# A fused attention and feed-forward kernel: the opening loads, tables and warm-up rearranged, and two blocks of the first chunk moved behind the second

## The chip, the cores and the metric

The program runs on one core of one Trainium2 chip. The metric is the device time of one execution in microseconds, and less is better. The core has a matrix engine (PE, with a loader of its stationary operands, PEld), a vector engine (DVE), a scalar engine (ACT), a general engine (POOL), and a queue engine (SP) that issues most of the DMA transfers.

## What is computed

Windowed causal attention with a distance bias, and a feed-forward layer on its output, all in float32:

```
B, H, S, D = 8, 8, 576, 64;  window = 128
scores = q k^T / sqrt(D) + slope_h * -|rel|, only for 0 <= rel < window
attn   = softmax(scores)                      # minus the row maximum, sum + 1e-9
x      = (attn v), heads side by side         # 4608 tokens x 512
h = x @ w_in                                  # 512 -> 2048
g = h * erf(softplus(h))
out = g @ w_out                               # 2048 -> 512
```

## The kernel before

The 4608 tokens are cut into 12 chunks of 384 tokens. Chunk c has four attention units, u = 4c to 4c+3, each for two heads. In each group of three chunks the last (units 8 to 11, 20 to 23, ...) joins the tails of two batches. Of a unit, PE makes the scores `s` (L464), DVE adds the bias and finds the row minimum (L491, six instructions and six small reads of accumulators), ACT takes the exponentials (L501), DVE inverts the sums (L514, L515), POOL scales the probabilities `p` (L524), PE transposes them into `t` (L543), DVE or ACT copies `t` into `pT`, PE multiplies by the values into `px` (L576), ACT or DVE writes the rounded half of x, and DVE the rest of x (L586), which is the last reader of `px`.

Products of the feed-forward layer are made in three passes of rounded operands (high by high, high by low, low by high). The first pass over the chunks uses the first six of the 16 column blocks of w_in and w_out: per chunk and block, 12 products into `h` (L783, six for each half of x), then softplus and erf on ACT, the split of g on DVE (L825 to L830), and nine products into three accumulators `o0` to `o2` (L846). After a chunk's sixth block the accumulators are copied and stored to DRAM (`keep_part`). The remaining ten blocks are worked in a second pass (L985, L1056), which loads these parts again and adds them (`store`).

The weights arrive as 64-bit floats. Each block of w_in or w_out is decoded by one ACT instruction and five DVE instructions (L621, L623, L625, L626, L631; tiles `wqi`, `wti`, for w_out `wqo`, `wto`), rounded (L638), and its remainder taken on DVE (L641). Twelve such blocks are prepared at the start of the kernel, beside the first attention units.

PE writes into PSUM banks: three under the tag `a` (scores, transposes and `px`), two for `h`, three for `o`. While the `h` and `o` banks are still unused, the scores of the first SPARE units go there (`early`). The scores of a unit that joins two batches take three banks, from unit 8 on all three `a` banks at once:

```
        ps = [bank(j) for j in range(2 + (last and len(ts) == 3))]
```

The order of the instructions on each engine is not that of the code. `Plan.run` is a list scheduler that runs when the program is built: it keeps modelled clocks of the engines and the DMA, and at each moment gives an engine the ready operation with the smallest `at`, if its buffers are free. The `at` of a unit is `unit_time(u)`, that of first-pass work counts up from LEAD in steps of TM, that of the weights is set in `prepare`. On the chip each engine then runs its list strictly in order, and an instruction that waits holds up all behind it on that engine. The warm-up products (L397, 40 pairs of matmuls on zeros) have the largest `at` and fill moments in which PE has nothing else.

Of the kernel before, what the change touches and what calls it, by code (L numbers as in the profile page):

```python
# [44 lines left out]
LL, LN, LT = 26, 0, 0  # L45
SQ = 0.36
# [59 lines left out]
class Plan:  # L106
# [254 lines left out]
class Attention:  # L361


    def __init__(self, tc, plan, ctx, actx, qk, v, bias, ident, moe):
        self.nc, self.plan = tc.nc, plan
        self.qk, self.v = qk, v
        self.ident, self.moe = ident, moe
        nc, op = self.nc, plan.op
        sb = lambda name: actx.enter_context(tc.tile_pool(name=name, bufs=1))
        biases = sb("biases")  # L370
        self.bias = []
        rel = Buf(shape=[P, 4, D], ap=biases.tile([P, 4, D], F32, name="rel"))
        op(emit=lambda e: nc.scalar.dma_start(rel.all, bias), w=[rel], at=-9, **dma(P * 4 * D * 4, run=1024, eng="Act"))
# [32 lines left out]
    def load(self, u):  # L406


        c, g = u // 4, u % 4
        nc, op = self.nc, self.plan.op  # L410
        at = unit_time(u) - LL
        last = c % 3 == 2
        n, m = (640, 10) if last else (448, 6)
        i = c // 3 if last else c - c // 3
        src, vsrc = self.qk[last][i, g], self.v[last][i, g]
        qk = Buf(self.kp, [P, CH + 640], F32, "qk", NKB, f"qk{u}")
        v = Buf(self.vp, [P, 10, 2, D], F32, "v", NQ, f"v{u}")
        rows = lambda j: slice(j * D, (j + 1) * D)
        q = lambda t, j, h: qk[rows(j), t * P + h * D : t * P + (h + 1) * D]
        k = lambda j, x, w: qk[rows(j), CH + x : CH + x + w]  # L420
        if u:
            parts = [[qk]] * 3
            op(emit=lambda e: nc.sync.dma_start(qk[:, : CH + n], src), w=[qk], at=at, **dma(P * (CH + n) * 4, run=(CH + n) * 4))
        else:
            pieces = [Part(qk, i) for i in range(4)]
            for i, (eng, issue, lo, hi) in enumerate((
                    ("SP", nc.sync, 0, P), ("Act", nc.scalar, CH, CH + 192), ("Act", nc.scalar, CH + 192, CH + n), ("SP", nc.sync, P, CH))):
                op(emit=lambda e, issue=issue, lo=lo, hi=hi: issue.dma_start(qk[:, lo:hi], src[:, lo:hi]), w=[pieces[i]], at=-30 + i,
                   **dma(P * (hi - lo) * 4, run=(hi - lo) * 4, eng=eng))
# [288 lines left out]
class Moe:  # L718
# [117 lines left out]
    def products(self, u, j, gh, gl):  # L836
# [363 lines left out]
```

## Time and profile before

| | us |
|---|---|
| three runs | 1003.12, 1003.21, 1004.44 |
| median | 1003.21 |
| the profiled execution | 1003.54 |
| its span, first to last instruction | 1001.5 |
| PE busy | 987.4 |
| DVE busy | 687.2 |
| ACT busy | 666.8 |
| POOL busy | 157.1 |

The span is cut into stretches below, since shares over the whole span mix stages with different limits. The chain of waits goes back from the last instruction to what released each step, so it names the engine that set the pace at each moment. The granted clock is 1.00 of full speed in all 40 slices of the span that the page shows, and the rows' PEclk is that of the clock record, which begins some 5 us into the span.

### The profile page before, as it was taken

How to read it: one execution, taken by the hardware profiler on the slowest of the kernel's cores; microseconds unless marked ns; L12 is line 12 of the kernel's file. 1: busy time of each engine (PE TensorE's matmuls, PEld its weight loads, DVE VectorE, ACT ScalarE, POOL GpSimd, SP SyncE). 2: the span in 40 equal slices, each digit the busy share in tenths (PEclk: the TensorE clock that was granted, in tenths of full speed). 3: DMA queues.
4: the chain of work that ended last, by engine and by line, in shares of the span. 5: the costliest groups of instructions: out<-in, count | busy, mean ns of one | idle time of the engine just before them, and what ended most of it. 6: DMA issues, size and time to landing. Idle time of an engine off the chain costs nothing.

```text
span 1001.5 us, 17129 instructions
## 1 busy us (share of the span) xinstructions
PE 987.4 (99%) x6188; PEld 876.5 (88%) x6188; DVE 687.2 (69%) x1635; ACT 666.8 (67%) x1259; POOL 157.1 (16%) x294
## 2 busy tenths in 40 slices
PE   8899999999999999999999999999999999999998
PEld 7788988988888898888999898998989989889896
DVE  5999988999988966575647367457547547544433
ACT  6899788778788787667866555555455464564652
POOL 3543333223332532022000000000000000000000
PEclk9999999999999999999999999999999999999999
DMA  9654577768776754562985252241342441420402
GB/s 360 250 173 165 198 258 253 274 232 322 264 233 220 269 175 138 176 211 84 346 320 187 81 189 88 70 175 67 105 158 64 126 152 48 147 95 1 127 1 73
DMA packets 63508, 172.17 MB, mean 172 GB/s; under 512 B 7104, under 2 KB 7744, under 8 KB 63424
## 3 DMA queue, kind: packets, MB, share of 16 engines
q1 hardware_dynamic: 62992, 170.72, 49.1%
q8 instruction: 49, 0.80, 0.3%
q10 hardware_dynamic: 432, 0.36, 0.1%
q14 instruction: 35, 0.29, 0.1%
HBM read 118.88 MB, written 52.17 MB: 171 GB/s over the span
## 4 chain that ended last, share of the span: by engine, by line
PE 92%; DVE 5%; ACT 1%; DMA 1%; issue 1%; POOL 0%; POOLq 0%; DVEq 0%; ACTq 0%
PE o L846 15%; PE h L783 14%; PE pa L985 13%; PE po L1056 12%; PE pa L1056 12%; PE px L576 7%; PE pc L985 6%; PE s L464 5%; PE t L543 4%; PE pb L985 3%; DVE p L491 1%; PE warm_ps L397 1%; DMA wd<-wto 1%; ACT p L501 1%; POOL p L524 0%
## 5 line engine op out<-in xcount | busy, mean ns | idle before, releaser
L524 POOL TENSOR_SCALAR p<-p,st 128x192 f32<-128x192 f32 (+1 forms) x288 | 156.4, 563 | 305.2 <-DVE st L515 224.0
L783 PE MATMUL h<-x,wi 128*128 128x384 f32 x864 | 173.9, 343 | 0.1
L766 ACT COPY hs<-pa 128x384 f32<-128x384 f32 x93 | 44.7, 481 | 177.3 <-PE pa L985 176.7
L783 PEld LDWEIGHTS h<-x,wi 128*128 128x128 f32 x864 | 149.5, 188 | 8.8 <-issue 4.7
L501 ACT ACTIVATE p<-p,st 128x192 f32<-128x192 f32 (+1 forms) x288 | 124.1, 434 | 32.1 <-DVE st L491 31.9
L846 PE MATMUL o<-wo,gh 128*128 128x512 f32 x432 | 142.0, 410 | 0.0
L985 PE MATMUL pa<-t,p 128*128 128x384 f32 x540 | 108.9, 336 | 0.0
L576 PEld LDWEIGHTS px<-pT,v 128*128 128x128 f32 x704 | 101.2, 191 | 5.1 <-issue 1.1
L576 PE MATMUL px<-pT,v 128*128 128x192 f32 (+2 forms) x704 | 102.9, 295 | 0.7 <-ACT pT L402 0.6
L985 PEld LDWEIGHTS pa<-t,p 128*128 128x128 f32 x540 | 96.4, 188 | 5.9
L768 DVE COPY hs<-pa 128x384 f32<-128x384 f32 x27 | 15.1, 557 | 111.3 <-PE pa L985 111.3
L1056 PE MATMUL po<-ho,gh 128*128 128x512 f32 x270 | 91.0, 391 | 0.0
L1056 PE MATMUL pa<-ho,gh 128*128 128x512 f32 x270 | 90.5, 389 | 0.0
L846 PEld LDWEIGHTS o<-wo,gh 128*128 128x128 f32 x432 | 74.9, 189 | 13.5 <-issue 5.0
L846 PE MATMUL o<-wo,gl 128*128 128x512 f32 x216 | 85.4, 395 | 0.0
L1056 PE MATMUL po<-ho,gl 128*128 128x512 f32 x180 | 71.3, 396 | 0.0
L1056 PE MATMUL pa<-ho,gl 128*128 128x512 f32 x180 | 70.1, 389 | 0.0
L491 DVE CUSTOM_DVE_ANT_0 p<-s,bias 128x192 f32<-128x192 f32 x224 | 66.0, 350 | 5.2 <-PE s L464 4.8
L996 DVE TENSOR_TENSOR hs<-pc,hs 128x384 f32<-128x384 f32 x60 | 33.3, 555 | 52.0 <-PE pc L985 39.2
L1036 DVE TENSOR_TENSOR hs<-s,hs 128x768 f32<-128x768 f32 x60 | 56.3, 950 | 16.9 <-ACT s L1028 16.9
L543 PE MATMUL t<-ident,p 128*128 128x128 f32 x400 | 61.4, 275 | 4.8 <-POOL p L524 3.2
L464 PE MATMUL s<-qk 64*64 64x192 f32 (+1 forms) x1152 | 59.7, 322 | 3.3 <-ACT pT L402 0.8
(257 smaller groups left out, 1851.7 us busy)
## 6 DMA issues: line engine op xcount, KB each, us to landing
xd<-x SPq DMA_DIRECT2D x24, 768.0 KB, 5.6
qk<-qk_a SPq DMA_DIRECT2D x31, 416.0 KB, 4.6
v<-v_a SPq DMA_DIRECT2D x32, 384.0 KB, 3.8
v<-v_c SPq DMA_DIRECT2D x16, 640.0 KB, 4.0
pd<-ot SPq DMA_DIRECT2D x36, 256.0 KB, 3.2
out<-pd SPq DMA_DIRECT2D x36, 256.0 KB, 3.8
p<-wd SPq DMA_DIRECT2D x35, 256.0 KB, 5.0
wri<-w_in SPq DMA_DIRECT2D x16, 512.0 KB, 7.0
```

The costliest lines, as they stand in the source:

```text
L464: nc.tensor.matmul(bank[h * D : (h + 1) * D, x : x + n], lhsT=q(t, j, h), rhs=k(j, off[h], n), start=True, stop=True)
L491: nc.vector.tensor_tensor_reduce(out=pt[:, c0:, j, :], in0=ps[j][0][:, ps[j][1] : ps[j][1] + n].rearrange("p (c d) -> p c d", d=D), in1=se ...
L501: nc.scalar.activation(dst, dst, AF.Exp, bias=low[t][:, j : j + 1], scale=-1.0, accum_out=sums[t][:, j : j + 1])
L524: nc.gpsimd.tensor_scalar(dst, dst, sums[t][:, j : j + 1], 1.0, op0=ALU.mult, op1=ALU.mult)
L543: nc.tensor.matmul(two[:, :, (2 - cb) * D : (3 - cb) * D], lhsT=p[t][:, cb].rearrange("p j d -> p (j d)"), rhs=self.ident[:, :], is_transp ...
L576: nc.tensor.matmul(px[:, to : to + m * D], lhsT=v[:, blk].rearrange("p j d -> p (j d)"), rhs=run(src, m, 256)[:, :, :D], start=first and x ...
L766: self.nc.scalar.copy(out, src)
L783: nc.tensor.matmul(ps[:, :CH], lhsT=ww[:, cs], rhs=xx[:, k], start=(k2 + k + n == 0), stop=(k2 + k + n == 4),)
L846: nc.tensor.matmul(po.all, lhsT=g[:, j, cs], rhs=w.all, start=(u["start"] and n == 0), stop=(u["end"] and n == 2),)
L985: nc.tensor.matmul(dst[:, :CH], lhsT=wv[i](k), rhs=xb[l][:, k], start=start and k + n == 0, stop=k + n == 3, skip_group_check=not start)
L1036: op({"DVE": dve(2 * CH)}, lambda e, s=s, hs=hs: V.tensor_tensor(hs.all, s.all, hs.all, ALU.mult), r=[s, *parts], w=parts, at=at, port=True)
L1056: nc.tensor.matmul(po.all, lhsT=g[:, k, cs], rhs=w.all, start=start and n == 0, stop=end and n == 2)
```

## The change

- **First loads.** Unit 0's q and k come in one load on SP where four went over two queues; the bias pattern `rel` goes first on ACT's queue. The loads of q and k of units 0 to 3 are placed ahead of all others, and the values' loads have times of their own (VE, VL).
- **Bias tables.** ACT multiplies `rel` by the slopes for head pair 0 alone; POOL makes the tables of pairs 1 to 3, two instructions each.
- **Warm-up and banks.** The warm-up has 30 pairs of matmuls where 40 were, in bank `o1`. Five early units where four were, and a table TURN says which banks each of them takes.
- **p buffers.** Nine where eight were.
- **Pace of the units.** `unit_time` counts 4 us for each of the first 6 units and 6.5 for each after, where it was 4.5 for the first 10.
- **Turns.** Chunk 0 does blocks 0 to 3, then chunk 1 blocks 0 to 5, then chunk 0 blocks 4 and 5. Each of chunk 0's two turns fills the accumulators anew; at the second, `keep_part` loads the part that was stored at the first, adds it on DVE, and stores the sum.
- **The planner's model** counts 0.3 us where it counted 1.5 for what waits on a load that lands before its time 9 (TS).

```
-SPARE = 4
+SPARE = 5
-WARM = 40
+WARM = 30
-NQ, NKB, PB, XB, OB, TB = 2, 4, 8, 5, 5, 2
-TE, NE = 4.5, 10
+NQ, NKB, PB, XB, OB, TB = 2, 4, 9, 5, 5, 2
+TE, NE = 4, 6
+TURNS = ((0, 0, 4), (1, 0, 6), (0, 4, 6))
+TS, VL, NQF, SLP = 9, 8, 4, True
+WB, PIE = "o1", 2
+VE = -17
+TURN = (0, 1, 2, 1, 2, 1, 2, 1)
...
-            return 0.14 + LM
+            return 0.14 + (LM if o.end + o.lag > TS else 0.3)
...
-        op(emit=lambda e: nc.scalar.dma_start(rel.all, bias), w=[rel], at=-9, ...
+        op(emit=lambda e: nc.scalar.dma_start(rel.all, bias), w=[rel], at=-40, ...
...
-                    nc.scalar.mul(b[:, j], rel.all, 2.0 ** (2 - 2 * g - j))
-            op({"Act": 2 * act(4 * D)}, slopes, r=[rel], w=[b], at=unit_time(g) - LL + 6)
+                    slope = 2.0 ** (2 - 2 * g - j)
+                    if e == "Act":
+                        nc.scalar.mul(b[:, j], rel.all, slope)
+                    else:
+                        nc.gpsimd.tensor_scalar(b[:, j], rel.all, slope, 1.0, op0=ALU.mult, op1=ALU.mult)
+            op({"Pool": 2 * (0.24 + 4 * D * 0.00086)} if SLP and g else {"Act": 2 * act(4 * D)}, slopes, ...
...
-        banks = (...)[u % 3 if early else 0]
+        banks = (...)[TURN[u] if early else 0]
...
-        for c in range(self.nch):
+        begun = {c for c, _, _ in TURNS}
+        for c, lo, hi in [*TURNS, *((c, 0, NF1) for c in range(self.nch) if c not in begun)]:
...
-            for f in fs:
+            for f in fs[lo:hi]:
+                u["more"] = lo > 0
...
-        op({"DVE": dve(DM), "Act": act(DM, src=0.053)},
-           lambda e: self.copy(e, ot.all, po.all), r=[po], w=[ot], at=at)
+        if more:
+            op(emit=lambda e: nc.sync.dma_start(ot.all, part.ap), r=[part], w=[ot], at=at - 10, ...
+            op({"DVE": dve(DM)}, lambda e: nc.vector.tensor_tensor(
+                ot.all, po.all, ot.all, ALU.add), r=[po, ot], w=[ot], at=at)
+        else:
+            op({"DVE": dve(DM), "Act": act(DM, src=0.053)}, ...
```

With these numbers the scheduler writes another order on every engine. Three places follow, each before and now. The digits behind a name are the unit (s9, px8), the block (wo2) or the count of the chunk-and-block pairs (h6); the number after the underscore is a running one.

ACT at the start, before: the first loads and tables, then the exponentials of units 0 and 1 (p0, p1), then the first steps on the weights (wqi).

```order
L428 DMA qk0_230<-qk_a 128x256
L373 DMA rel_152<-bias 128x256
L379 ACTIVATE bias0_153<-rel_152 128x256 x2
L379 ACTIVATE bias1_154<-rel_152 128x256 x2
L379 ACTIVATE bias2_155<-rel_152 128x256 x2
L379 ACTIVATE bias3_156<-rel_152 128x256 x2
L501 ACTIVATE p0_0_304,st0_305<-p0_0_304,st0_305 128x2x64 x2
```

ACT at the start, now, from the load of `rel` to the first weight steps.

```order
L378 DMA rel_152<-bias 128x256
L386 ACTIVATE bias0_153<-rel_152 128x256 x2
L511 ACTIVATE p0_0_291,st0_292<-p0_0_291,st0_292 128x2x64 x2
L511 ACTIVATE p0_1_312,st0_292<-p0_1_312,st0_292 128x3x64 x2
L511 ACTIVATE p0_2_317,st0_292<-p0_2_317,st0_292 128x3x64 x2
L511 ACTIVATE p1_0_338,st1_339<-p1_0_338,st1_339 128x2x64 x2
L511 ACTIVATE p1_1_346,st1_339<-p1_1_346,st1_339 128x3x64 x2
L511 ACTIVATE p1_2_350,st1_339<-p1_2_350,st1_339 128x3x64 x2
L511 ACTIVATE p2_0_360,st2_361<-p2_0_360,st2_361 128x2x64 x2
L511 ACTIVATE p2_1_372,st2_361<-p2_1_372,st2_361 128x3x64 x2
L511 ACTIVATE p2_2_382,st2_361<-p2_2_382,st2_361 128x3x64 x2
L628 ACTIVATE wqi0_438<-wri0_245 128x512
```

Three tables are gone from ACT, and three units' exponentials stand ahead of the first weight step where two did.

DVE up to the x that unit 9's scores wait for, before: that of unit 7 (px7).

```order
L631 TENSOR_TENSOR wto1_983<-wto1_983,wqo1_965 128x512
L626 SCALAR_TENSOR_TENSOR wqo2_985<-wro2_388,wqo2_985 128x512
L638 CAST wo1_1094<-wto1_983 128x512
L825 TENSOR_TENSOR hs2_930<-s2_1013,hs2_930 128x768
L641 TENSOR_TENSOR wo1_1094<-wto1_983,wo1_1094 128x512
L631 TENSOR_TENSOR wto2_1017<-wto2_1017,wqo2_985 128x512
L514 TENSOR_SCALAR st8_1033<-st8_1033 128x6
L515 RECIPROCAL st8_1033<-st8_1033 128x6
L586 TENSOR_TENSOR x1_1_977<-px7_1085,x1_1_977 128x384
```

DVE up to the x that unit 9's scores wait for, now: that of unit 8 (px8).

```order
L641 TENSOR_TENSOR wto2_1060<-wto2_1060,wqo2_1049 128x512
L636 SCALAR_TENSOR_TENSOR wqo3_1051<-wro3_511,wqo3_1051 128x512
L648 CAST wo2_1128<-wto2_1060 128x512
L641 TENSOR_TENSOR wto3_1062<-wto3_1062,wqo3_1051 128x512
L651 TENSOR_TENSOR wo2_1128<-wto2_1060,wo2_1128 128x512
L648 CAST wo3_1136<-wto3_1062 128x512
L631 TENSOR_SCALAR wto4_1138<-wqo4_1115 128x512
L651 TENSOR_TENSOR wo3_1136<-wto3_1062,wo3_1136 128x512
L633 SCALAR_TENSOR_TENSOR wto4_1138<-wqo4_1115,wto4_1138 128x512
L596 TENSOR_TENSOR x2_0_1149<-px8_1117,x2_0_1149 128x384
```

Unit 8's x now stands between unit 7's and unit 9's scores, and blocks 2 and 3 of w_out, with steps of block 4, stand ahead of it.

PE just ahead of unit 9's scores, before.

```order
L586 MATMUL px7_1085<-pT7_1069,v7_896 128x64
L846 MATMUL o2_0_1100<-wo0_981,gh0_960 128x512 x2
L846 MATMUL o2_0_1100<-wo0_981,gl0_967 128x512
L783 MATMUL h7_1108<-x1_0_821,wi1_580 128x384 x6
L846 MATMUL o0_0_1071<-wo1_1094,gh0_960 128x512 x2
L846 MATMUL o0_0_1071<-wo1_1094,gl0_967 128x512
L464 MATMUL s9_02_1135<-qk9_656 64x192
```

PE just ahead of unit 9's scores, now.

```order
L586 MATMUL px8_1117<-pT8_1087,v8_1011 128x64
L795 MATMUL h5_982<-x1_1_1020,wi1_654 128x384 x6
L795 MATMUL h6_1152<-x1_0_907,wi2_726 128x384 x6
L474 MATMUL s9_02_1162<-qk9_609 64x192
L474 MATMUL s9_01_1164<-qk9_609 64x192
```

Unit 8's `px` has moved ahead of unit 9's scores, with one half of a chunk-and-block pair between it and them that needs nothing of unit 8; the transposes of unit 8 have moved ahead with it.

## Rows read from the trace of the kernel before

**Rows 1.** The page: busy time of each engine (us, share of the span, instructions), and the chain that ended last by engine.

```profile
PE 987.4 (99%) x6188; PEld 876.5 (88%) x6188; DVE 687.2 (69%) x1635; ACT 666.8 (67%) x1259; POOL 157.1 (16%) x294
...
PE 92%; DVE 5%; ACT 1%; DMA 1%; issue 1%; POOL 0%; POOLq 0%; DVEq 0%; ACTq 0%
```

**Rows 2.** The chain of waits in order of time, 0 to 130 us: start, us, engine and tile, line, instructions merged.

```profile
1.05 6.28 PE warm_ps L397 x38
...
16.00 0.86 DVE wti L621 x2
...
78.62 2.38 PE px L576 x20
...
82.45 1.10 PE h L783 x6
...
86.29 0.70 PE o L846 x3
...
88.05 0.98 PE t L543 x9
```

**Rows 3.** Busy time of each engine by stretch: length, PE, PEld, DVE, ACT, POOL (each with its instructions), granted clock, DMA share, GB/s.

```profile
17.50:60.80 43.30, 37.92 (x317) 32.08 (x315) 43.09 (x147) 35.60 (x110) 22.56 (x38) 1.00 0.77 277
60.80:72.00 11.20, 11.09 (x80) 9.65 (x80) 11.16 (x32) 11.05 (x24) 3.92 (x7) 1.00 0.35 119
72.00:120.00 48.00, 47.67 (x381) 41.39 (x384) 47.73 (x141) 43.91 (x100) 19.21 (x29) 1.00 0.50 172
```

**Rows 4.** The timeline of PE: the scores of unit 8 and of unit 9, and a transpose at 155 us; in brackets the idle time ahead and what ended it.

```profile
60.78 1.55 PE L464 MATMUL s<-qk 64*64 64x192 f32 x24 [0.70 <-DVE x L586]
...
72.03 1.55 PE L464 MATMUL s<-qk 64*64 64x192 f32 x24
...
155.81 0.41 PE L543 MATMUL t<-ident,p 128*128 128x128 f32 x2 [0.92 <-DVE x L586]
```

**Rows 5.** The timeline of all engines at the start: the bias tables, unit 0's scores, bias and exponentials, unit 1's exponentials, the first weight steps on ACT and DVE, unit 2's bias.

```profile
6.67 2.56 ACT L379 ACTIVATE bias<-rel 128x256 f32<-128x256 f32 x8 [4.65 <-DMA rel<-bias]
...
7.27 1.10 PE L464 MATMUL s<-qk 64*64 64x128 f32 x24
...
8.53 0.29 DVE L491 CUSTOM_DVE_ANT_1 p<-s,bias 128x128 f32<-128x128 f32 x1 [7.53 <-PE s L464]
...
9.13 0.39 ACT L501 ACTIVATE p<-p,st 128x128 f32<-128x128 f32 x1
...
12.54 0.40 ACT L501 ACTIVATE p<-p,st 128x128 f32<-128x128 f32 x1 [0.79 <-DVE st L491]
...
15.08 1.26 ACT L618 ACTIVATE wqi<-wri 128x512 f32<-128x512 f32 x2
...
15.92 0.94 DVE L621 TENSOR_SCALAR wti<-wqi 128x512 int32<-128x512 int32 x2
...
17.53 0.28 DVE L491 CUSTOM_DVE_ANT_1 p<-s,bias 128x128 f32<-128x128 f32 x1
```

**Rows 6.** The warm-up's matmuls alone, by stretch: length, PE busy, PEld busy, granted clock, DMA share, GB/s.

```profile
1.00:4.83 3.83, 3.78 (x18) 3.78 (x18) 1.00 0.70 198
4.83:7.26 2.43, 2.43 (x23) 2.31 (x21) 1.00 1.03 401
```

**Rows 7.** DMA issues of the first 3 us: tile, queue, size, us from issue to landing (the whole load of unit 1's q and k; the load of `rel`).

```profile
qk<-qk_a SPq DMA_DIRECT2D x1, 416.0 KB, 5.4
...
rel<-bias ACTq DMA_DIRECT2D x1, 128.0 KB, 5.0
```

**Rows 8.** DVE's groups by line and form, 17.5 to 72 us: busy us, mean ns of one, idle time ahead.

```profile
L641 DVE TENSOR_TENSOR wi<-wti,wi 128x512 fp32r<-128x512 f32 x6 | 4.5, 742 | 0.0
L631 DVE TENSOR_TENSOR wti<-wti,wqi 128x512 f32<-128x512 f32 x6 | 4.4, 733 | 0.0
L623 DVE SCALAR_TENSOR_TENSOR wti<-wqi,wti 128x512 int32<-128x512 int32 x6 | 4.3, 718 | 0.0
L626 DVE SCALAR_TENSOR_TENSOR wqi<-wri,wqi 128x512 f32<-128x512 uint32 x6 | 4.3, 717 | 0.0
...
L638 DVE CAST wi<-wti 128x512 fp32r<-128x512 f32 x5 | 2.6, 523 | 0.0
...
L621 DVE TENSOR_SCALAR wti<-wqi 128x512 int32<-128x512 int32 x4 | 1.9, 479 | 0.0
```

**Rows 9.** The timeline of DVE: the first instruction after a unit's bias, a short weight step and what follows it, and the stretch up to the x of unit 7.

```profile
19.06 0.41 DVE L404 COPY pT<-t 128x256 f32<-128x256 f32 x1
...
21.20 0.41 DVE L625 TENSOR_SCALAR wqi<-wti 128x512 int32<-128x512 int32 x1
21.54 0.54 DVE L404 COPY pT<-t 128x384 f32<-128x384 f32 x1
...
70.38 0.68 DVE L631 TENSOR_TENSOR wto<-wto,wqo 128x512 f32<-128x512 f32 x1
70.98 0.15 DVE L514 TENSOR_SCALAR st<-st 128x6 f32<-128x6 f32 x1
...
71.28 0.52 DVE L586 TENSOR_TENSOR x<-px,x 128x384 fp32r<-128x384 f32 x1
71.72 0.55 DVE L638 CAST wo<-wto 128x512 fp32r<-128x512 f32 x1
```

**Rows 10.** POOL's scaling of the probabilities by form, 0 to 60 us: busy us, mean ns of one.

```profile
L524 POOL TENSOR_SCALAR p<-p,st 128x192 f32<-128x192 f32 x28 | 16.7, 614 | 0.0
```

More of the change, by code (lines that the diff above doesn't have):

```diff
@@ L372, in __init__ @@
         rel = Buf(shape=[P, 4, D], ap=biases.tile([P, 4, D], F32, name="rel"))
-        op(emit=lambda e: nc.scalar.dma_start(rel.all, bias), w=[rel], at=-9, **dma(P * 4 * D * 4, run=1024, eng="Act"))
+        op(emit=lambda e: nc.scalar.dma_start(rel.all, bias), w=[rel], at=-40, **dma(P * 4 * D * 4, run=1024, eng="Act"))
         for g in range(NPAIR):
@@ L378, in slopes @@
                 for j in range(2):
-                    nc.scalar.mul(b[:, j], rel.all, 2.0 ** (2 - 2 * g - j))
-            op({"Act": 2 * act(4 * D)}, slopes, r=[rel], w=[b], at=unit_time(g) - LL + 6)
+                    slope = 2.0 ** (2 - 2 * g - j)
[3 more added lines that the diff above has]
+                        nc.gpsimd.tensor_scalar(b[:, j], rel.all, slope, 1.0, op0=ALU.mult, op1=ALU.mult)
+            op({"Pool": 2 * (0.24 + 4 * D * 0.00086)} if SLP and g else {"Act": 2 * act(4 * D)}, slopes, r=[rel], w=[b], at=unit_time(g) - LL + 6)
             self.bias.append(b)
@@ L422, in load @@
             parts = [[qk]] * 3
-            op(emit=lambda e: nc.sync.dma_start(qk[:, : CH + n], src), w=[qk], at=at, **dma(P * (CH + n) * 4, run=(CH + n) * 4))
+            op(emit=lambda e: nc.sync.dma_start(qk[:, : CH + n], src), w=[qk], at=u - 29 if u < NQF else at, **dma(P * (CH + n) * 4, run=(CH + n) * 4))
         else:
[L425 to L428, printed above, removed]
+            pieces = [Part(qk, i) for i in range((4, 2, 1)[PIE])]
+            for i, (eng, issue, lo, hi) in enumerate(((
+                    ("SP", nc.sync, 0, P), ("Act", nc.scalar, CH, CH + 192), ("Act", nc.scalar, CH + 192, CH + n), ("SP", nc.sync, P, CH)),
+                    (("SP", nc.sync, 0, CH), ("SP", nc.sync, CH, CH + n)), (("SP", nc.sync, 0, CH + n),))[PIE]):
+                op(emit=lambda e, issue=issue, lo=lo, hi=hi: issue.dma_start(qk[:, lo:hi], src[:, lo:hi]), w=[pieces[i]], at=-40 + i,
                    **dma(P * (hi - lo) * 4, run=(hi - lo) * 4, eng=eng))
             parts = [pieces[:2], pieces, pieces]
-        op(emit=lambda e: nc.sync.dma_start(v[:, :m].rearrange("p x j d -> p (x j d)"), vsrc), w=[v], at=at + 2,
+        op(emit=lambda e: nc.sync.dma_start(v[:, :m].rearrange("p x j d -> p (x j d)"), vsrc), w=[v], at=VE + 2 * u if u < NQF else at + VL,
            **dma(P * m * 2 * D * 4, run=m * 2 * D * 4))
@@ L439, in scores @@
         last = u // 4 % 3 == 2
-        banks = ((self.ps, "a", "a", 3, 0), (self.moe.ps_h, "h", "h", 2, None), (self.moe.ps_o, "o0", "o2", 1, None))[u % 3 if early else 0]
+        banks = ((self.ps, "a", "a", 3, 0), (self.moe.ps_h, "h", "h", 2, None), (self.moe.ps_o, "o0", "o2", 1, None))[TURN[u] if early else 0]
         pool, *tags, bufs, keep = banks
@@ L744, in first_pass @@
         fs = weights.ffs
-        for c in range(self.nch):
+        begun = {c for c, _, _ in TURNS}
+        for c, lo, hi in [*TURNS, *((c, 0, NF1) for c in range(self.nch) if c not in begun)]:
             x = [(self.x[c][k2], [b for g in (2 * k2, 2 * k2 + 1) for b in self.x_parts[c][g]]) for k2 in range(2)]
             po = [Buf(self.ps_o, [P, DM], F32, f"o{t}", 1, f"o{t}_{self.U}") for t in range(NTT)]
-            for f in fs:
-                u = self.unit(c, f, weights, x, po, f == fs[0], f == fs[-1], time(self.U))
+            for f in fs[lo:hi]:
+                u = self.unit(c, f, weights, x, po, f == fs[lo], f == fs[hi - 1], time(self.U))
+                u["more"] = lo > 0
                 self.round.append(u)
@@ L852, in products, with keep_part @@
             if u["end"]:
-                self.keep_part(self.part[u["c"]][t], po, at)
-    def keep_part(self, part, po, at):
+                self.keep_part(self.part[u["c"]][t], po, at, u["more"])
+    def keep_part(self, part, po, at, more):
         nc, op = self.nc, self.plan.op
         ot = Buf(self.op_, [P, DM], F32, "o", OB, "ot")
-        op({"DVE": dve(DM), "Act": act(DM, src=0.053)},
-           lambda e: self.copy(e, ot.all, po.all), r=[po], w=[ot], at=at)
+        if more:
+            op(emit=lambda e: nc.sync.dma_start(ot.all, part.ap), r=[part], w=[ot], at=at - 10, **dma(P * DM * 4, run=2048))
+            op({"DVE": dve(DM)}, lambda e: nc.vector.tensor_tensor(
+                ot.all, po.all, ot.all, ALU.add), r=[po, ot], w=[ot], at=at)
+        else:
+            op({"DVE": dve(DM), "Act": act(DM, src=0.053)},
+               lambda e: self.copy(e, ot.all, po.all), r=[po], w=[ot], at=at)
         op(emit=lambda e: nc.sync.dma_start(part.ap, ot.all), r=[ot], w=[part], at=at, **dma(P * DM * 4, run=2048, out=True))
```

2 lines of the change are left out of this document (1 added, 1 removed).

## The prediction

> **What bounds the kernel now.** I read the page first, then the chain, then the stretches, then the timelines. On the page PE is busy for 99% of the span and the chain gives it 92% [rows 1]: nothing helps that doesn't let PE start sooner or idle less. The chain in order of time shows where PE isn't in charge: it is in the warm-up to about 7.3 us, leaves to DVE at 16.0, and is held by PE's own products from unit 8 on [rows 2]. The stretches say the same: from 17.5 to 60.8 us DVE is busy for 43.09 of 43.30 us and PE for 37.92; from 72 on PE is busy for 47.67 of 48 [rows 3]. The last wait of that early phase is 0.70 us ahead of unit 8's scores, at 60.78, for an x on DVE; unit 9's scores follow at 72.03 with no idle time named, and the only large wait that I found later is 0.92 us at 155.81 [rows 4]. The profiled run took 1003.54 us, of which 1001.5 is the span, and stands 0.33 us above the median of 1003.21; I work out a shift and add it to the median. So the question is when unit 9's scores begin, and how much PE has done by then. After that PE's work is the same list in another order.
>
> **The start.** Unit 0's scores wait for the warm-up: 38 of its matmuls stand in the chain ahead of them [rows 2]. Now it is 14 pairs, 28 matmuls. The first 18 took 3.78 us, the next 20 the 2.43 us to 7.26 [rows 6], 0.12 us each; so 28 end at 4.83 + 10 x 0.12 = 6.05, and the scores begin at 6.05 where it was 7.27 [rows 5]. The load must have landed: as one load of q and k it takes the 5.4 us of unit 1's, and `rel` 5.0 [rows 7]; issued in the first 0.8 us they land by 6.2 and 5.8. Head pair 0's bias is two instructions where eight take 2.56 us [rows 5], 0.64, done by 6.5, ahead of DVE's first bias at about 7.3. The landing is worth +-0.5 us.
>
> POOL's tables are six instructions of 256 elements. POOL's scaling of 192 elements takes 614 ns [rows 10], so I estimate 0.82 us each, 4.9 in all, done by 10.7 us; the first is needed at about 9.4, when two are done. POOL has nothing else before 12 us, and I count nothing; without that cover it is at most 0.8 us, within the half us above. The values' loads are asked for later, but the first `px` comes after 16 us: hidden.
>
> ACT's first exponentials come 1.86 us after the scores (9.13 - 7.27), so at 7.9. A unit of them takes 2.54 (12.54 to 15.08) [rows 5]; now three units stand ahead of the first weight step, 7.9 + 7.6 = 15.5, the two steps take 1.26, and DVE's first two weight steps end at about 17.3. There DVE begins the fourth unit's bias, where before it began the third's at 17.53 [rows 5]. DVE is one unit further on and 0.23 us early.
>
> **Unit 8.** It comes sooner. Counting PE's products ahead of its scores by the durations of their rows, it is 3.8 us less, and DVE's list up to the x that they wait for (now unit 5's) ends at about 54.9 by the spacings used below. So the scores begin 5.9 us earlier with 3.8 us less done: PE is 2.1 us ahead. That would be the gain if nothing came after it.
>
> **Unit 9, the gate.** Its scores need all three `a` banks. Before, unit 7 held the last, and its x began at 71.28 and let go 0.44 later, at 71.72 [rows 9], ahead of PE's 72.03. Now `px8` stands ahead of them, and unit 8's x must be done. From 17.3 us on I add what DVE has in its list up to there against what it had from 17.53 to 71.72. Spacings, start to start, are those of rows 9 unless another group is named.
>
> Less: the bias of one unit, 1.53 (17.53 to 19.06) [rows 5, 9]; one inverse, 0.30 (70.98 to 71.28); three short copies of pT at 0.34 and one long at 0.44; together 3.3 us.
>
> More: the x of unit 8, a cast and a rest at 0.44; one g, twice the 384 columns, which I put at 0.88; together 1.8. And 13 weight steps: 2 of L621, 3 of L623, 1 each of L625, L626 and L631, 3 of L638, 2 of L641. In the clear a slow step (L623, L626, L631, L641) occupies 0.60 us (70.38 to 70.98) and a fast one 0.34 (21.20 to 21.54), so 7 x 0.60 + 6 x 0.34 = 6.2. By the groups' means over the stretch, 733 ns where the clear one has 0.68, they are 0.48 to 0.74 us each [rows 8]; less 0.08 of overlap with the next, 7.05. The sum is -3.3 + 1.8 + 6.2 or 7.05, 4.7 to 5.5; I take 5.1, in the middle, since POOL works beside DVE in about half the stretch (22.56 of 43.30) [rows 3].
>
> So unit 8's x ends at 71.72 - 0.23 + 5.1 = 76.6, 4.9 us after unit 7's did. DVE has no idle time to give here: in 60.8 to 72 it was busy for 11.16 of 11.20 [rows 3]. What of this PE can fill: it will have done unit 8's transposes (0.98) and `px8` (2.38) more, and one half of h (1.10) and one triple of o (0.70) less [rows 2], 1.56 more. The rest is idle: 4.87 - 1.56 = 3.3 us. The 2.1 us won at unit 8 is spent by then, since PE runs out of work that it may do: one half of h stands between `px8` and the scores, and what could fill the time stands behind them.
>
> One page speaks to the hold-ups in those means. Rows 8 and 9 show the step L641 and its like longer on average than in the clear. The Trainium skill, "SBUF — State Buffer", section "Who interferes with whom", says that DVE and GpSimd share a pair of ports under an exclusive lock; the trace has the longer means but doesn't name their cause. By that rule one unit of scaling less beside DVE would take away some 0.3 us of the 5.1, which my bounds hold.
>
> **After the gate.** The weights are ready some 6 us of DVE's work earlier against the rest of the list, so the wait of 0.92 at 155.81 [rows 4] may go; bounds 0 and 0.92, I take half, -0.45. Chunk 0's second turn adds three loads, and three additions on DVE in place of three copies of the same width: the loads stand 10 us of planned time ahead, and like those of rows 7 land within 5 us or so. PE waits for these sums only when it needs the same accumulators again. I count nothing; if each of the three sums were late by a fast step it would be up to 0.8 us with the next joining unit's gate, kept as an upper bound. The ninth p buffer, the bank of the warm-up and the planner's constant have no cost of their own on the chip; they act through the order counted above.
>
> **Sum.** 3.3 - 0.45 = +2.85, and 1003.21 + 2.85 = 1006.1. Bounds: steps +-0.4, start +-0.5, later -0.5 to +0.8; together 1004.2 to 1007.8. A measurement of this kernel tells about 0.2% from no change, so "same" is 1001.2 to 1005.2.
>
> **Rivals.**
> - *Faster: DVE doesn't gate unit 9.* Then the 2.1 us at unit 8 stays, and 1003.2 - 2.1 - 0.45 = 1000.7. For it: PE is 99% busy and what starts sooner ends sooner. It needs unit 8's x by 76.6 - 3.3 - 2.1 = 71.2, 5 us earlier than the count; DVE was full in that stretch, and the steps would have to cost nearly nothing. Against that stand rows 3 and 8.
> - *Same: the hold-ups vanish and the start is better.* With steps at the clear price (-0.4), the start 0.5 us earlier, the hold-ups shrunk and the later wait gone altogether (-0.5), +2.85 becomes about +1 or less: 1003.9. The decisive point is an x of unit 8 that ends before about 75.
> - *Slower still: the clock.* The granted clock is 1.00 in the rows that I have, 2.4 GHz, in the warm-up and from 17.5 us on [rows 3, 6]. The warm-up is now ten pairs shorter and PE has gaps after it; if the clock fell to 1.2 GHz between 13 and 26 us, PE's products there, some 10 us, would take up to twice as long. Most of it lies beside DVE's chain; bounds 0 and 4 us, I take 2: 1008.1. It decides if the granted clock of that stretch is 0.5. The Trainium skill, "TensorE: Matmul & The Clock Gate", section "Part 4: PE-mode transpose", says that a transpose doesn't count as a busy PE in the same way, which would favour this; rows 3, at 1.00, don't.
> - *The change doesn't do what it says:* the one load lands late and unit 0's scores begin at 7.3 still. Then the gate moves by up to 1.2 us: 1007.3, inside the range.
>
> **Chances.** Forecast 0.44, some of its low end counted as same; faster rival 0.20; same 0.24; clock 0.08; late load 0.04. From these: faster 0.23, same 0.29, slower 0.48. The range reaches down to the faster rival less its start's bound, 1000.3, and up to the clock's 1008.1; beyond it I leave some 0.15.
>
> **What would show it.** Right: unit 0's scores at about 6.1; unit 3's bias on DVE at about 17.3; unit 8's scores near 55; unit 9's scores the longest idle time of PE after 60 us, 2 us or more, released by DVE's x near 76.6; DVE busy throughout to there. Wrong: unit 8's x done by 73, or no idle time on PE ahead of unit 9's scores; a wait of that size elsewhere, at the sums of chunk 0 for instance; a granted clock under 1.00 after 13 us.

## The result, and the profile after

The changed kernel takes 1009.51 us (median of four, 1009.10 to 1010.46) where the kernel before took 1003.2: a ratio of 1.0061, 95% interval 1.0048 to 1.0073. It is slower by some 6.2 us, and the forecast of 1006.1 with a range up to 1008.1 was too low. The profiled run has a span of 1007.3 us where before it was 1001.5.

The page of the changed kernel: busy time of each engine, and the chain that ended last by engine.

```profile
PE 986.4 (98%) x6168; PEld 875.3 (87%) x6168; DVE 686.5 (68%) x1636; ACT 665.6 (66%) x1255; POOL 154.7 (15%) x300
...
PE 90%; DMA 5%; DVE 3%; issue 1%; POOL 1%; ACT 1%; SPq 0%; POOLq 0%; DVEq 0%; ACTq 0%
```

The engines are busy for nearly the same time as before [rows 1], and the span is 5.8 us longer. So it is idle or slow time of PE, and one looks for where. The timeline of PE in the changed kernel shows the places: unit 0's scores, px of units 4 and 5, unit 8's scores, the second part of unit 7's px, unit 8's transposes, its px, and unit 9's scores.

```profile
6.10 1.10 PE L474 MATMUL s<-qk 64*64 64x128 f32 x24
...
48.29 3.68 PE L586 MATMUL px<-pT,v 128*128 128x192 f32 x24 [1.42 <-issue]
...
54.64 1.68 PE L474 MATMUL s<-qk 64*64 64x192 f32 x24 [1.70 <-issue]
56.25 3.75 PE L795 MATMUL h<-x,wi 128*128 128x384 f32 x12
...
64.06 1.63 PE L586 MATMUL px<-pT,v 128*128 128x192 f32 x10 [0.65 <-ACT pT L411]
...
68.32 0.55 PE L553 MATMUL t<-ident,p 128*128 128x128 f32 x3 [1.88 <-POOL p L534]
...
71.72 0.90 PE L553 MATMUL t<-ident,p 128*128 128x128 f32 x3 [0.35 <-POOL p L534]
72.27 1.61 PE L795 MATMUL h<-x,wi 128*128 128x384 f32 x6
73.72 2.54 PE L586 MATMUL px<-pT,v 128*128 128x192 f32 x20
76.07 2.36 PE L795 MATMUL h<-x,wi 128*128 128x384 f32 x12
78.36 1.55 PE L474 MATMUL s<-qk 64*64 64x192 f32 x24
```

The start went as forecast: unit 0's scores at 6.10, unit 8's at 54.64, against 7.27 and 60.78 before [rows 4, 5]. Unit 9's scores begin at 78.36, 6.3 us later than before, and no wait stands ahead of them. The waits stand ahead of unit 4's px, unit 8's scores, unit 7's px and unit 8's own transposes. Adding all idle pieces of over 0.2 us between 44 and 100 us gives 6.23 us here, and 1.11 in the kernel before. Twelve products of h take 3.75 us at 56.25 and 2.36 at 76.07: the clock. The changed kernel by stretch: length, PE, PEld, DVE, ACT, POOL, granted clock, DMA share, GB/s.

```profile
52.00:54.00 2.00, 0.82 (x6) 0.38 (x4) 2.00 (x5) 2.00 (x8) 0.00 (x0) 1.00 0.75 242
54.00:56.00 2.00, 1.26 (x24) 0.77 (x24) 1.97 (x7) 1.97 (x4) 0.96 (x2) 0.98 0.18 71
56.00:59.00 3.00, 3.00 (x16) 2.75 (x10) 3.00 (x16) 2.95 (x4) 2.54 (x5) 0.50 0.46 142
59.00:69.00 10.00, 7.25 (x45) 6.16 (x44) 9.19 (x19) 7.52 (x21) 3.01 (x3) 0.98 0.40 133
70.00:72.50 2.50, 2.15 (x9) 1.46 (x9) 2.50 (x5) 0.48 (x1) 1.66 (x2) 0.50 0.00 0
```

Twice, after PE was idle for over half of 52 to 54 us and for 1.88 us ahead of 68.32, the granted clock is 0.50, the 1.2 GHz level, for some 3 us each. In the kernel before it was 1.00 there [rows 3]. The trace gives the 1.70 us ahead of unit 8's scores as "issue". In DVE's list the last step ahead of them is unit 5's x, and DVE's timeline has it just before they begin at 54.64:

```profile
53.99 0.55 DVE L596 TENSOR_TENSOR x<-px,x 128x384 fp32r<-128x384 f32 x1
```

POOL's timeline in the changed kernel, unit 7's scaling and unit 8's:

```profile
55.04 3.51 POOL L534 TENSOR_SCALAR p<-p,st 128x128 f32<-128x128 f32 x6 [10.29 <-DVE st L525]
65.99 5.67 POOL L534 TENSOR_SCALAR p<-p,st 128x192 f32<-128x192 f32 x6 [7.45 <-DVE st L525]
```

And DVE's, around unit 8's x:

```profile
65.72 0.65 DVE L651 TENSOR_TENSOR wo<-wto,wo 128x512 fp32r<-128x512 f32 x1
...
76.81 0.56 DVE L596 TENSOR_TENSOR x<-px,x 128x384 fp32r<-128x384 f32 x1 [0.60 <-ACT x L411]
```

Unit 8's six scalings take 5.67 us while DVE works on weights beside them from 65.72 on, and the chain of waits goes through them to unit 8's last transposes:

```profile
66.89 4.78 POOL p L534 x5
...
71.72 0.90 PE t L553 x3
```

Unit 8's x ends at 76.81 + 0.48 = 77.3, close to the forecast 76.6; but DVE had waited 0.60 us for it, and PE did not wait for it.

### The profile page after: what moved, and what is told of

The parts are those of the page before. It is cut to its first block, busy times and chain, and to the rows that moved or that the text cites. A ratio compares the mean times of both kernels' runs of the same rounds, so it can differ in the third digit from the quotient of the medians.

```text
span 1007.3 us, 17103 instructions
## 1 busy us (share of the span) xinstructions
PE 986.4 (98%) x6168; PEld 875.3 (87%) x6168; DVE 686.5 (68%) x1636; ACT 665.6 (66%) x1255; POOL 154.7 (15%) x300
## 4 chain that ended last, share of the span: by engine, by line
PE 90%; DMA 5%; DVE 3%; issue 1%; POOL 1%; ACT 1%; SPq 0%; POOLq 0%; DVEq 0%; ACTq 0%
PE h L795 14%; PE o L858 14%; PE pa L1004 13%; PE po L1075 12%; PE pa L1075 12%; PE px L586 8%; PE pc L1004 6%; PE s L474 4%; PE t L553 4%; PE pb L1004 3%; DMA wro<-w_out 1%; DMA wd<-sb 1%; DMA wri<-w_in 1%; DMA qk<-qk_c 1%; POOL p L534 1%
## 5 line engine op out<-in xcount | busy, mean ns | idle before, releaser
L534 POOL TENSOR_SCALAR p<-p,st 128x192 f32<-128x192 f32 (+1 forms) x288 | 151.6, 545 | 304.6 <-DVE st L525 210.4
L795 PE MATMUL h<-x,wi 128*128 128x384 f32 x864 | 176.4, 346 | 0.0
L553 PEld LDWEIGHTS t<-ident,p 128*128 128x128 f32 x400 | 48.6, 144 | 20.2 <-POOL p L534 10.0
```

The costliest lines, as they stand in the source:

```text
L534: nc.gpsimd.tensor_scalar(dst, dst, sums[t][:, j : j + 1], 1.0, op0=ALU.mult, op1=ALU.mult)
L553: nc.tensor.matmul(two[:, :, (2 - cb) * D : (3 - cb) * D], lhsT=p[t][:, cb].rearrange("p j d -> p (j d)"), rhs=self.ident[:, :], is_transp ...
L795: nc.tensor.matmul(ps[:, :CH], lhsT=ww[:, cs], rhs=xx[:, k], start=(k2 + k + n == 0), stop=(k2 + k + n == 4),)
```

## The experiments

Medians below are beside a kernel before of 1003.0 to 1003.5 us on the same chip. In kernels with a hook, the planned order is taken as it is and only what the diff names is moved.

**The turns alone undone (e1).**

```diff
-TURNS = ((0, 0, 4), (1, 0, 6), (0, 4, 6))
+TURNS = ()
```

> The changed kernel with the turns alone undone: chunk 0 does its six blocks in one turn. Its list on PE is that of the changed kernel up to unit 8, but ahead of unit 9's scores stands unit 7's px and not unit 8's. Theory A (the loss is made by what the turns put ahead of unit 9's scores: unit 8's p, t, px and x, and the weight steps among them): the start's lead of some 2 us stays, 1000.5 to 1003. Rival (the loss comes from the new start, its pace of units, loads and buffers): 1006 or more.

1000.99 us, ratio 0.9979 (0.9970 to 0.9987): faster than both kernels. The new start gives 2 to 2.5 us, and the turns cost 8.2 to 8.5. PE's timeline of e1, unit 6's last transposes to unit 9's scores:

```profile
54.02 1.13 PE L553 MATMUL t<-ident,p 128*128 128x128 f32 x6
54.91 2.36 PE L795 MATMUL h<-x,wi 128*128 128x384 f32 x12
57.20 1.55 PE L474 MATMUL s<-qk 64*64 64x192 f32 x24
58.68 2.37 PE L795 MATMUL h<-x,wi 128*128 128x384 f32 x12
...
70.16 1.55 PE L474 MATMUL s<-qk 64*64 64x192 f32 x24
```

Between unit 6's transposes and unit 8's scores stand the 12 products of chunk 0's block 4, and behind the scores those of block 5; there is no idle time. (This profiled run took 1002.79 us, 1.8 more than the median of e1: unit 0's scores begin at 7.31, and the granted clock was 0.50 from 28 to 34 us.)

**The turns alone, with the start of before (e2).** All constants but TURNS as before, and the first loads and tables.

> The kernel before with the turns alone added. The scheduler puts unit 9's scores behind unit 7's px here, not behind unit 8's. Theory A (place of unit 8's px, not the turns in themselves): within 3 us of 1003.2, and no idle time of 1.5 us on PE ahead of unit 8's transposes. Rival B (the two turns cost by themselves, by three sums more, later gates and blocks in another order): 1007 or more.

1010.34 us, ratio 1.0069 (1.0057 to 1.0082). Theory A falls: unit 8's px is behind unit 9's scores here, and the turns cost 6.9 us all the same, at a granted clock of 1.00. PE's timeline of e2, unit 8's scores and two products of o:

```profile
61.40 1.55 PE L474 MATMUL s<-qk 64*64 64x192 f32 x24 [1.81 <-DVE x L596]
...
69.92 0.51 PE L858 MATMUL o<-wo,gh 128*128 128x512 f32 x1 [0.51 <-DVE wo L648]
71.59 0.50 PE L858 MATMUL o<-wo,gh 128*128 128x512 f32 x1 [1.16 <-DVE wo L651]
```

The wait for unit 5's x is there again, and PE runs into blocks of w_out that DVE has not made.

**Zeros in the waits (e3, e5).** Products on zeros ahead of unit 4's px, unit 8's scores and unit 8's first transposes; in e3 10, 12 and 15, in e5 5, 6 and 7.

```diff
+filler(bank o1, n)        # ahead of px4: 10 / 5; ahead of s8: 12 / 6
+filler(columns 384 on of t8_0's bank, n)   # ahead of t8_0: 15 / 7
```

> The changed kernel with 37 products on zeros more on PE, in three places where it waited: 10 ahead of unit 4's px (idle 1.42 us there), 12 ahead of unit 8's scores (1.70), 15 ahead of unit 8's first transposes (1.88). Theory C (the granted clock of 0.50 in 56 to 59 and 70 to 72.5 us follows from those waits and its slow products stand on the path): clock 1.00 throughout, and 1 to 2.2 us less than the changed kernel, 1007.3 to 1008.5. Rival (the path runs over DVE and POOL there, and the slow products are hidden): clock 1.00 but at most 0.4 us less, 1009.1 or more.

1010.11 us: no gain, though its last three runs had a granted clock of 1.00. The edit was too big: a product of two float32 operands is two matmuls, and 10 of them took 2.39 us where 1.42 were idle. So it says nothing for or against theory C.

> The changed kernel with 18 products on zeros on PE, 5, 6 and 7 in the three places where it waited 1.42, 1.70 and 1.88 us. Each is two matmuls of 0.12 us, so they fill 1.2, 1.4 and 1.7 us and fit (the 37 of the run before took 2.4, 2.9 and 3.5 us and pushed unit 8's scores back). Theory C (the slow products at a granted clock of 0.50 stand on the path): clock 1.00 from 50 to 80 us and 0.8 to 2 us less than the changed kernel, 1007.5 to 1008.7. Rival (they are hidden behind POOL's scaling): less than 0.5 us, 1009 or more.

1008.05 us, 1.5 us less than the changed kernel (1.2 by the ratios, whose intervals overlap), with some 4.5 us of work more. The slow clock is on the path, and costs about that. PE's timeline of e5, a stretch, and then the waits that are left ahead of unit 8's transposes:

```profile
65.14 1.72 PE L1271 MATMUL t<-warm 128*128 128x128 f32 x14
67.16 0.55 PE L554 MATMUL t<-ident,p 128*128 128x128 f32 x3 [0.30 <-POOL p L535]
...
70.55 0.55 PE L554 MATMUL t<-ident,p 128*128 128x128 f32 x3 [1.12 <-POOL p L535]
```

Its granted clock by stretch:

```profile
50.00:60.00 10.00, 9.42 (x81) 8.43 (x81) 9.96 (x31) 9.91 (x20) 3.50 (x6) 1.00 0.41 124
60.00:70.00 10.00, 7.52 (x48) 6.14 (x46) 9.97 (x21) 6.95 (x21) 5.17 (x6) 1.00 0.39 131
```

PE reaches unit 8's last transposes sooner and waits 1.12 us there for POOL where it waited 0.35.

**Weight steps behind unit 8's x (e4).**

```diff
+steps = DVE's weight steps between unit 8's inverse and its x   # 17 of them
+order = resort(order, steps, behind=x of unit 8)
```

> The changed kernel with 17 of DVE's weight steps (blocks 1 to 4 of w_out) moved from between unit 8's inverse and its x to right behind that x, and with them two decoding steps of ACT. Theory A (these steps delay unit 8, by their place ahead of x on DVE and by holding up POOL's scaling): the scaling takes 3.3 to 3.7 us and not 5.67, unit 9's scores begin 2 to 4 us earlier, 1005.5 to 1007.5. Rival (the steps are owed anyway and PE waits for the blocks of w_out later): within 0.8 us of the changed kernel.

1015.5 us, 6 us worse. The near half of theory A holds and the far half doesn't. POOL's timeline of e4:

```profile
66.08 3.21 POOL L534 TENSOR_SCALAR p<-p,st 128x192 f32<-128x192 f32 x6 [6.58 <-ACT wqo L628]
```

and PE's:

```profile
75.42 1.55 PE L474 MATMUL s<-qk 64*64 64x192 f32 x24
...
81.56 3.91 PE L795 MATMUL h<-x,wi 128*128 128x384 f32 x12 [3.33 <-ACT hs L778]
...
87.28 1.58 PE L474 MATMUL s<-qk 64*64 64x192 f32 x24 [1.81 <-issue]
```

With DVE's steps away from it the same scaling takes 3.21 us, and unit 9's scores begin 2.9 us sooner, at 75.42. But the steps are owed: ACT's decoding, which had to move with them, holds a copy of h on ACT, and PE waits 3.33 us for it; the 1.81 us behind that have no cause named in the trace. This edit moved two things, so only its first part is read.

**Unit 8's scaling on ACT (e6), and with the zeros (e9).**

```diff
-nc.gpsimd.tensor_scalar(dst, dst, sums[t][:, j : j + 1], 1.0, op0=ALU.mult, op1=ALU.mult)
+if u == 8: nc.scalar.mul(dst, dst, sums[t][:, j : j + 1])
```

> The changed kernel with unit 8's scaling of p, six instructions, on ACT and not on POOL; all lists else stand as they were, DVE's weight steps too. ACT has some 3.8 us of idle time there. Theory P (POOL's scaling, stretched to 5.67 us beside DVE, holds unit 8's transposes, its px and all behind them): the six take 2 to 3 us, unit 8's last transposes begin near 70 and not at 71.7, unit 9's scores 1.5 to 2.5 us earlier, 1007 to 1008. Theory A (the count of DVE's steps ahead of unit 8's x is the gate by itself): that x still ends at 76 or later, PE waits for it ahead of unit 9's scores, and the gain is under 1 us.

1006.77 us, 2.7 us less than the changed kernel (2.5 by the ratios). ACT's timeline of e6, the six scalings:

```profile
68.82 0.80 ACT L535 ACTIVATE p<-p,st 128x192 f32<-128x192 f32 x2
...
69.88 1.50 ACT L535 ACTIVATE p<-p,st 128x192 f32<-128x192 f32 x4
```

PE's, unit 8's first transposes and unit 9's scores:

```profile
69.67 0.55 PE L556 MATMUL t<-ident,p 128*128 128x128 f32 x3 [1.06 <-ACT p L535]
...
78.15 1.55 PE L474 MATMUL s<-qk 64*64 64x192 f32 x24 [0.29 <-DVE x L599]
```

Theory P holds: POOL's scaling is worth 2.7 us, and this includes one of the two slow stretches, since the granted clock is 1.00 from 66 to 80 us here. Now, and only now, PE waits for the x that I had named, by 0.29 us: DVE's count is a second gate right behind the first. (This profiled run lies 2.1 us later than the changed kernel's: unit 8's scores begin at 56.78, and 78.15 answers to 76.0.)

> The changed kernel with both edits together: 18 products on zeros where PE waited, and unit 8's scaling on ACT. If the two costs (clock 1.5 us, POOL's scaling 2.7 us, by the two runs with one of them) stand one behind the other, 1005.0 to 1005.8; if they are the same time counted twice, 1006.5 or more.

1007.04 us: the two gains don't add up, and together they are 2.5 us. With the scaling on ACT one of the two slow stretches is gone already (e6); and the idle time that the zeros fill ahead of the transposes is 1.06 us, and they take 1.7.

**The turn late, and one block instead of two (e7, e8).**

```diff
+TURNS = ((0, 0, 6), (1, 0, 6), (2, 0, 6), (3, 0, 6), (4, 0, 4), (5, 0, 6), (4, 4, 6))   # e7
+TURNS = ((0, 0, 5), (1, 0, 6), (0, 5, 6))                                              # e8
```

> The new start without the turns of chunks 0 and 1 (run e1), and the same kind of turn much later: chunk 4 does blocks 0 to 3, chunk 5 blocks 0 to 5, chunk 4 blocks 4 and 5. No weights of the first pass are decoded there. Theory S (the turns cost because they put off PE's ready work in the phase in which DVE is full): within 1 us of e1, 1000 to 1002. Rival T (stores, loads and sums of the chunk that is worked in two turns cost by themselves): 1004 or more.

1001.23 us, ratio 0.9985 (0.9976 to 0.9994): 0.2 us above e1 by the medians and 0.6 by the ratios, whose intervals overlap. So at this place the sums, loads and stores cost nothing that can be told from noise. Up to unit 9's scores and beyond, this kernel has e1's lists, and its profiled run wasn't held up. POOL's timeline of e7, unit 8's scaling:

```profile
65.47 4.77 POOL L534 TENSOR_SCALAR p<-p,st 128x192 f32<-128x192 f32 x6 [7.24 <-DVE st L525]
```

PE's, unit 9's scores:

```profile
67.59 1.55 PE L474 MATMUL s<-qk 64*64 64x192 f32 x24
```

Without the turns unit 8's p is ready at 70.2 us, with them at 71.7: nearly the same. What differs is PE, which has other work until then, and unit 9's scores among it.

> The changed kernel with one block of chunk 0 put off instead of two: blocks 0 to 4, then chunk 1, then block 5. The sums, loads and stores are the same as in the changed kernel. Unit 8's px stands behind unit 9's scores again. Theory S (the cost grows with the work that is put off, two halves of h for each block): about half of the 8.2 us between e1 and the changed kernel, 1004 to 1006.5. Rival A (the place of unit 8's px ahead of unit 9's scores makes it): 1000.5 to 1003. Rival T (the sums): 1008 or more.

1005.88 us, 4.9 us above e1: somewhat over half of the cost for half of the work, with unit 8's px behind unit 9's scores. Its transposes stand ahead of them still, so the place of these is tested by e2 alone, with the start of before. Idle time of PE between 44 and 100 us is 4.46 us, its largest piece here:

```profile
71.37 0.55 PE L553 MATMUL t<-ident,p 128*128 128x128 f32 x3 [1.89 <-POOL p L534]
```

**A lighter DVE (e10, e11).** Two of five decoding steps of each of the first pass's twelve blocks are left out.

> The changed kernel, with two of the five decoding steps on DVE (the sign, L633, and the low words, L636) left out for each of the twelve blocks of weights of the first pass, 24 steps of 0.60 us or 14.4 us of DVE; the weights are then not the true ones. Read against the next kernel, which is the same without the turns. Theory S (the turns cost because DVE is full there and PE's products wait for what it makes): the difference between the two falls from 8.5 us to under 4. Rival (the turns cost by PE's order and its banks alone): it stays at 7 or more.

> Without the turns, and with the same 24 decoding steps left out. Theory S: PE's waits in the first 120 us shrink by 2 to 5 us, 996 to 999.5, and the kernel with the turns stands less than 4 us above it. Rival: 7 us or more above it.

1005.71 us with the turns and 996.62 without: 9.1 us apart. Some of this is the clock, whose mean was 0.995 to 0.998 in e10's runs and 0.999 or 1.000 in e11's; but e10's fastest run, 1003.40, is 6.8 us above e11 too. So the cost of the turns is not that DVE is full. PE's timeline of e10 has three waits of the changed kernel to the hundredth:

```profile
51.42 2.51 PE L474 MATMUL s<-qk 64*64 64x192 f32 x24 [1.70 <-issue]
...
60.77 1.63 PE L586 MATMUL px<-pT,v 128*128 128x192 f32 x10 [0.65 <-ACT pT L411]
...
65.03 0.80 PE L553 MATMUL t<-ident,p 128*128 128x128 f32 x3 [1.88 <-POOL p L534]
```

though DVE is idle for 3 of the 10 us from 50 on:

```profile
50.00:60.00 10.00, 8.27 (x58) 6.70 (x58) 6.96 (x25) 9.91 (x20) 2.58 (x6) 0.83 0.27 81
```

POOL's scaling of unit 8 begins 11.3 us after unit 8's scores in both kernels (62.71 and 51.42, 65.99 and 54.64). Ahead of it stand ACT's exponentials of unit 8, which end 10.2 to 10.3 us after these scores in both; a lighter DVE doesn't bring them sooner, and no run here shortens ACT's part.

**The cover taken away without the turns (e13).**

```diff
+h = PE's products of chunk 0's block 4 ahead of unit 8's scores   # 12 products
+order = resort(order, h, behind=scores of unit 8)                 # on e1
```

> The new start without the turns (run e1), with one edit on PE: the 12 products of chunk 0's block 4 go from ahead of unit 8's scores to right behind them; they are done 1.5 us later, and no list else changes. Theory K (cover: those products hide the wait for unit 5's x, and the turns took them away): PE waits 1.5 to 1.9 us ahead of unit 8's scores, as in the changed kernel, and the time is 0.8 to 2 us above e1, 1001.8 to 1003. Rival (PE has room behind, the wait costs nothing): within 0.5 us of e1's 1001.0.

1004.98 us, ratio 1.0016 (1.0008 to 1.0025), 4.0 us above e1 and by the ratios 3.7: the wait that theory K names, but twice its price and outside its range. PE's timeline of e13:

```profile
55.27 1.54 PE L474 MATMUL s<-qk 64*64 64x192 f32 x24 [1.71 <-issue]
56.74 4.45 PE L795 MATMUL h<-x,wi 128*128 128x384 f32 x24
61.84 1.93 PE L586 MATMUL px<-pT,v 128*128 128x192 f32 x12 [0.65 <-PE h L795]
...
71.39 1.55 PE L474 MATMUL s<-qk 64*64 64x192 f32 x24
```

The same products, 1.5 us later, and the wait of the changed kernel is there. Counted from unit 0's scores, at 6.73 in this profiled run and at 5.76 in that of e7, unit 9's scores come 2.8 us later than in e7, and 1.71 + 0.65 is most of that. That the medians are 4.0 us apart I have not explained: in most of its runs the mean granted clock was 0.997 or 0.998, where in most of e1's it was 1.000, but its three runs at 1.000 took 1004.4 to 1005.1 too.

**Both gates shorter, with the turns (e14).** e10 with unit 8's scaling on ACT.

> The changed kernel with 24 decoding steps left out of DVE's list (so not the true weights) and unit 8's scaling on ACT: both ways to unit 9's scores made shorter, DVE's count and POOL's scaling. Read against 996.62, the same without the turns and with POOL's scaling, and 1005.71, the same with the turns and POOL's scaling. Theory K: PE still has nothing to do while unit 8's a banks and copies come round, so 5 us or more of the 9.1 stay, 1001.6 to 1003.5. Rival (the two gates side by side, DVE and POOL, are the whole cost): 1000 or less.

1002.81 us, 6.2 us above e11, as theory K has it: with both gates shorter most of the turns' cost stays. With DVE light, the scaling on ACT is worth 2.9 us, of which a part is the lower clock of e10's runs.

**A wait moved (e12).** On e1, five weight steps from among unit 7's bias on DVE to behind it.

> The new start without the turns (run e1), with one edit on DVE: the five weight steps that stand between the first and the last bias of unit 7 go right behind the last. In e1 PE waits 1.42 us ahead of unit 4's px, for a bank that unit 7's bias holds. If that wait is on the path, it goes and the kernel is 0.7 to 1.4 us faster than e1, 999.6 to 1000.4; if the steps that come 2 us later (a block of w_in) are waited for instead, within 0.5 us of 1001.0 or slower.

1002.28 us: no gain over e1's 1000.99. The 1.42 us ahead of unit 4's px are gone, and PE waits 2.01 us two steps on, in e12's timeline:

```profile
53.16 0.56 PE L553 MATMUL t<-ident,p 128*128 128x128 f32 x3 [2.01 <-DVE x L596]
53.44 3.90 PE L795 MATMUL h<-x,wi 128*128 128x384 f32 x12
```

The 12 products behind it run at the 1.2 GHz level (granted clock 0.50 from 54 to 56 us) and take 3.90 us. The clock seems to be all that it loses: its four runs at a mean of 0.999 or 1.000 took 1000.56 to 1001.29 us, e1's time, and the other eight 1002.25 to 1003.32.

Idle time of PE in pieces of over 0.2 us, between 44 and 100 us, added up from the timelines:

| kernel | median us | idle us |
|---|---|---|
| before | 1003.2 | 1.11 |
| e1, new start without turns | 1000.99 | 1.71 |
| e13, e1 with one cover moved | 1004.98 | 4.22 |
| e8, one block put off | 1005.88 | 4.46 |
| changed kernel, two blocks put off | 1009.51 | 6.23 |
| e11, light, without turns | 996.62 | 1.02 |
| e14, light, turns, scaling on ACT | 1002.81 | 4.43 |
| e10, light, turns | 1005.71 | 4.91 |

The idle time is not the whole cost: from e1 to the changed kernel it grows by 4.5 us, and the time by 8.2 to 8.5, of which the slow clock is 1.2 to 1.5.

## Why the prediction was wrong

- **The start: right.** 6.10 against 6.05 for unit 0's scores, 7.70 against 7.9 for ACT's first exponentials, 16.98 against 17.3 for unit 3's bias, 54.64 against 54.9 for unit 8's scores. That the first agrees to 0.05 us is luck: in the profiled runs with this start unit 0's scores begin between 5.76 (e7) and 7.31 us (e1), outside the 0.5 us allowed. The loads, POOL's tables and the late values cost nothing, as counted; the six tables took 2.46 us, half of the 4.9 estimated. The gain by itself was 2.1 and up to 0.45 more in the forecast; e1 measures 2.1 (by the ratio) to 2.5.
- **"Unit 9, the gate": the step that failed.** The sum took DVE's list up to unit 8's x as what PE waits for, 5.4 us from the lead of 2.1 to the loss of 3.3. The count of that list was right: DVE came to the x at 76.2 us, its begin in the sum too, and the x ended at 77.3 against 76.6. The PE work that had moved was right as well. The conclusion drawn from them was wrong in its cause and too small: between e1 and the changed kernel it is 8.2 to 8.5 us. I never asked when `px8` itself could run. It waits for unit 8's transposes, these for POOL's scaling. 2.2 of PE's 6.2 us of waiting stood there, the rest ahead of unit 4's px, unit 8's scores and unit 7's steps, and none ahead of unit 9's scores. In the sum's own terms, these scores came 6.33 us later than before and not 4.87, which less 1.56 is a loss of 4.8 and not 3.3; that the two are of one order is luck, since the wait that was counted didn't occur.
- **POOL was the wrong side of the hold-up.** I put the hold-ups down as a slower DVE, 0.3 us at stake. The wait was POOL's: 5.67 us for six scalings beside DVE's weight steps, 3.21 with them moved away (e4), and 2.5 to 2.7 us of the time (e6). The Trainium skill, "SBUF — State Buffer", section "Who interferes with whom", has DVE and GpSimd, which is POOL here, share a pair of ports under an exclusive lock. The runs agree with it on both sides: with POOL's scaling gone from that stretch (e6), the DVE steps that took 0.82 and 0.83 us take 0.69.
- **The clock rival came near its price by luck, and in the wrong place.** It was set at 13 to 26 us, for the shorter warm-up, at 2 us. There the granted clock stayed at 1.00. It fell at 56 and 70 us, behind the new waits, and costs 1.2 to 1.5 us (e5).
- **What the steps left out: cover.** POOL and clock together bring 2.5 of the 8.2 to 8.5 us (e9). The turns take the products of chunk 0's blocks 4 and 5 from between the steps of units 6 to 8. Their x was long done, so PE could run them while it waited for unit 5's x, for copies of pT and for unit 8's p, the last of which is ready at nearly the same time without the turns (e7). Moving block 4 by 1.5 us costs 3.7 to 4.0 (e13), putting off block 5 alone 4.9 (e8), both 8.2 to 8.5. So each block is shown to be cover by itself; that lost cover is all of the rest is argued from these sums. In the prediction this is one phrase, that one half of h stands between `px8` and the scores; I counted the PE work that had moved, 1.56 us, and not the waits that it had hidden.
- **After the gate.** I counted a gain of 0.45 for the wait at 155.81. PE waits 1.12 us at 154.18 in the changed kernel, for POOL. Nothing was gained there: of the 5.8 us between the spans some 1.0 was lost behind unit 9's scores. That the sums of chunk 0 are free is right: they run on DVE from 167.7 to 171.0 us, and the next wait of PE of over 0.2 us is at 345.38.
- **The range.** Its bounds as listed give 1004.7 to 1007.8, so the lower end of 1004.2 doesn't follow from them. The result lies above all of them, and above the 1008.1 of the clock rival.
- **Open.** How the lost cover, up to 6 us, splits over the single waits; why e13 costs more than its two waits; and what ACT's steps ahead of unit 8's p are worth, which no run shortened.

## What to carry to other kernels

Work whose inputs are long ready is cover: before it is moved, look up which waits it stands in front of, and price those, not the length of the work itself. When a gate is counted on one engine, walk the other way as well, from the last reader back through each engine that its data pass, and take the later of the two. A wait on a busy matrix engine can cost twice, once as idle time and once as a slower clock behind it. The version to keep is the new start without the turns, 1000.99 us.

## What the hardware showed that I had not expected

- Six scalings on POOL took 5.67 us beside DVE's weight steps and 3.21 us with these moved away (e4). One each of DVE's steps L633 and L636 took 0.82 and 0.83 us in that stretch, another L633 in it 0.68, and those behind it 0.68.
- The granted clock went to 0.50 for about 3 us at 56 and at 70 us, behind idle pieces of 1.70 and 1.88 us; with zeros in these pieces it stayed at 1.00. It doesn't follow each time: in the profiled runs of e13 and e8 the clock was 1.00 behind pieces of 1.71 and 1.89 us. And it isn't the same in every run: e1's profiled run had 0.50 from 28 to 34 us and a mean of 0.996, and eight of its eleven runs a mean of 1.000.
- One product of float32 operands of 128 columns shows as two matmuls of 0.12 us.
